# One small load on another queue, silu on another engine, and a new order of a written-out schedule

## The chip, the core and the metric

The kernel runs on one core of one Trainium2 chip. A core has five engines that run at the same time, each through its own list of instructions: TensorE (PE in the profile) multiplies matrices and writes to PSUM, VectorE (DVE), ScalarE (ACT) and GpSimd (POOL) work element by element, and SyncE (SP) issues the DMA transfers. They wait for each other by semaphores. The metric is the time of one execution on the device in microseconds (us).

## What is computed

One transformer block with adaptive layer norm, linear attention and a gated feed-forward part, on 2048 tokens of 512 channels, all in bfloat16:

```python
mod = (_silu(c) @ w_mod).reshape(c.shape[0], 6, 1, -1)
sa, ca, ga, sb, cb, gb = ...
h = _layernorm(x) * (1 + ca) + sa
x = x + ga * A(h)          # attention, 32 heads of 16 channels
h = _layernorm(x) * (1 + cb) + sb
x = x + gb * B(h)          # (silu(h @ w_gate) * (h @ w_up)) @ w_down, 1376 wide
```

In A, queries and keys go through a small matrix per head, `w_phi` (32 matrices of 16 by 16, 16 KB in all). phi of each is softmax(p) and softmax(-p) side by side, and the attention is num / den with num = phi_q (phi_k^T v) and den = phi_q (sum of phi_k). There is no product of tokens with tokens.

## The kernel before

**Staging.** Weights and all activations stay in SBUF. The 2048 tokens are 16 tiles of 128, in four chunks of x (`x_ch`). The stages are: preparation; K tiles (`k_tile`, `kv_tile`), which accumulate the key-value sums of all 16 tiles in `kv_ps`; Q tiles (`q_tile`); then, tile by tile, attention (`attend_tile`), its projection and second layer norm (`project`, `second_T`), and the feed-forward part (`ffn_gu`, `ffn_tail`, `ffn_down`) in six units of tokens. Stages overlap.

**Preparation**, which the change is mostly about:

- `c` is loaded through ACT's queue. Four products with a 1 by 1 matrix (`f_cT`, L450) turn it into a column in PSUM; ACT makes exp(-c) (L459); `f_silu` makes silu(c) with three operations of VectorE (L454 to L456).
- `mod_cols` (L471 and L473) multiplies silu(c) with the first third of `w_mod` as its four row blocks land, and a copy (L478) gives `modA`, the shift and scale of the first layer norm.
- `f_phx` (L499) spreads `w_phi` with 16 products of 16 columns, and VectorE makes the block-diagonal matrix `BD` from the result in PSUM (L502).
- `fold_phi` multiplies BD into the key weights (and later the query weights): 16 transposes of `wk` (L519), copies of them out of PSUM (L523), products with BD (L530), and copies back (L533, L534).
- `first_norm` takes the statistics of a tile of x (L348, L349), makes 1/sqrt(var) either by Ln and Exp of ACT (L377, L378) or by a power of GpSimd (L381, L382), and normalizes (L392, L396, L398 by engine). `turn_first` and `modulate_T` transpose (L563, L414) and apply modA on the way out of PSUM (L566, L567, L422).
- The first K product (L619) needs the folded wk and the modulated tokens.

**What sets the order.** Nothing is left to a scheduler of the compiler. Every step is recorded as an `Op` of a `Plan`, with what it reads and writes, an assumed duration (`us=`) and sometimes several engines to choose from (`alts`; "DVE*" is a VectorE operation that the plan keeps from running beside GpSimd). Loads recorded by `later` carry a size `kb` that the plan turns into a landing time, and a `Buf` with `at=` counts as ready at that time. The list `ORDER` gives the order in which the ops are placed: an entry divided by 4 is the op, and the remainder is the engine chosen. `Plan.run` walks it, gives each op a planned start, and the program is emitted in order of the planned starts. So the durations, sizes and `at=` in the code are assumptions that shape the order of instructions on each engine; on the chip the semaphores decide.

**Loads.** SP issues in this order: x chunk 0, wk, w_phi, w_mod (two row blocks, then one, then one), the two halves of x chunk 1, x chunk 2, wq, wv, x chunk 3, then transposes and the later weights.

**Filler.** Where the plan sees PE idle, `fill` puts products of a matrix of ones into the gap, which nothing reads; they keep PE busy. In the early part the number of columns is the gap times 1200 columns per us where the gap starts before 7.0 us, and 2400 behind it.

```python
left = int((o.start - t0) * (1200 if t0 < 7.0 else 2400))
while left >= 128:
    fns.append(lambda n=min(left, CW): f(n))
    left -= CW
```

## Time and profile before

| what | value |
|---|---|
| median of 3 runs | 199.06 us (199.02 to 199.08) |
| the profiled execution, its own time | 199.18 us |
| its span, first to last instruction | 197.4 us |
| granted TensorE clock | 1.000 of full speed |
| bytes read from and written to HBM | 11.58 MB and 2.10 MB |

The page of a profile shows, for each engine, the busy time, the groups of instructions that cost most, and the chain of work that ended last: from the last instruction back to what released each step. Besides it one can ask who waited for whom, what ran in a stretch of time, and when each transfer landed. In a line such as "L519 PE", the number is the line of the kernel. A stretch lists the busy time of PE, PEld (weight loads of PE), DVE, ACT and POOL, each with its number of instructions, then the granted clock, the busy share of the 16 DMA engines, and GB/s. Times in the text are from the start of the span.

When the first loads were issued and when they landed, by the trace:

| load | KB | issued by SP, us | landed, us |
|---|---|---|---|
| x chunk 0 | 512 | 0.72 | 4.1 |
| wk | 512 | 1.18 | 6.01 |
| w_phi | 16 | 1.65 | 6.2 |
| w_mod, row blocks 0 and 1 | 512 | 2.19 | 8.11 |
| w_mod, row block 2 | 256 | 2.7 | 8.79 |
| w_mod, row block 3 | 256 | 3.1 | 9.44 |

### The profile page before, as it was taken

The page shows a single profiled execution, that of the slowest core. Times are in us where ns is not written, and L with a number is a line of the kernel's source. Part 1 is how long each engine was busy: PE and PEld are TensorE (multiplying, and loading weights), DVE is VectorE, ACT ScalarE, POOL GpSimd, SP SyncE. Part 2 cuts the span into 40 slices and gives each one's busy share as a digit, 9 for nine tenths or more (in the row PEclk, how much of TensorE's full clock was granted, in tenths as well). Part 3 has the DMA queues.
Part 4 walks back from the last instruction along what each step waited for, and adds up shares of the span by engine and source line. Part 5 has one row for each costly group of instructions (what it writes and reads, how often), then busy time and mean ns, then how long its engine had stood idle before and what let it go on. Part 6 is the DMA issues. An engine that isn't in the chain of part 4 may idle for free.

```text
span 197.4 us, 4080 instructions
## 1 busy us (share of the span) xinstructions
PE 192.4 (97%) x1494; PEld 108.1 (55%) x1494; DVE 136.3 (69%) x268; ACT 108.9 (55%) x247; POOL 126.0 (64%) x207
## 2 busy tenths in 40 slices
PE   7999999999999999999999999999999999999993
PEld 2754555555754777967664555554444544544452
DVE  5999999999999899998973873844234203241453
ACT  2499999999769974366452452633145330134300
POOL 1469999999997667686763777657746420139200
DMA  6999789899928570836509157150370001021112
GB/s 203 334 381 151 129 201 355 186 310 392 203 53 162 107 151 13 167 66 110 99 14 188 37 100 82 30 130 0 66 103 20 27 0 53 3 66 40 47 38 76
DMA packets 51141, 24.16 MB, mean 122 GB/s; under 512 B 42449, under 2 KB 47922, under 8 KB 51122
## 3 DMA queue, kind: packets, MB, share of 16 engines
q1 hardware_dynamic: 50976, 23.88, 51.7%
q8 instruction: 11, 0.18, 0.4%
q14 instruction: 8, 0.07, 0.1%
q10 hardware_dynamic: 146, 0.03, 0.1%
HBM read 11.58 MB, written 2.10 MB: 69 GB/s over the span
## 4 chain that ended last, share of the span: by engine, by line
PE 93%; DMA 3%; DVE 1%; issue 1%; SPq 0%; DVEq 0%
PE one_ps L909 35%; PE one_ps L987 17%; PE one_ps L857 7%; PE one_ps L623 7%; PE one_ps L686 7%; PE one_ps L619 7%; PE one_ps L955 3%; DMA wk<-in_A_wqkv_dram 2%; PE kv_ps L663 2%; PE kv_ps L824 2%; PE kv_ps L1054 1%; DMA out_dram<-ot 1%; PE one_ps L530 1%; PE one_ps L473 1%; DVE fg L997 1%; PE one_ps L414 1%
## 5 line engine op out<-in xcount | busy, mean ns | idle before, releaser
L909 PE MATMUL one_ps<-hT,wgu_sb 128*128 128x512 bf16 (+2 forms) x480 | 74.5, 308 | 0.0
L909 PEld LDWEIGHTS <-wgu_sb 128*128 128x128 bf16 x480 | 40.3, 98 | 28.7
L916 ACT ACTIVATE sg<-one_ps 128x512 bf16<-128x512 f32 (+1 forms) x41 | 23.6, 586 | 37.2 <-PE one_ps L909 24.9
L987 PE MATMUL one_ps<-wd_sb,gu 128*128 128x512 bf16 (+1 forms) x160 | 37.8, 372 | 0.0
L925 POOL TENSOR_TENSOR gu<-usb,sg 128x512 bf16<-128x512 bf16 x19 | 22.1, 1168 | 24.2 <-ACT sg L916 12.2
L997 DVE TENSOR_TENSOR fg<-one_ps,gab 128x512 bf16<-128x512 f32 (+1 forms) x16 | 10.4, 667 | 23.8 <-PE one_ps L987 23.8
L919 DVE TENSOR_TENSOR gu<-one_ps,sg 128x512 bf16<-128x512 f32 (+1 forms) x22 | 14.2, 658 | 18.1 <-PE one_ps L909 11.1
L987 PEld LDWEIGHTS <-gu 128*128 128x128 bf16 x180 | 16.6, 98 | 16.0
L348 DVE BATCH_NORM_STATS2 st<-x_c 128x6 f32<-128x512 bf16 x32 | 21.3, 678 | 1.7 <-DMA x_c<-in_A_x_dram 1.5
L923 ACT CAST usb<-one_ps 128x512 bf16<-128x512 f32 x19 | 11.1, 586 | 18.2 <-PE one_ps L909 18.0
L640 DVE TENSOR_REDUCE S<-e 128x64 f32<-128x1024 bf16 x16 | 19.2, 1202 | 0.4 <-POOL e L657 0.2
L694 DVE TENSOR_REDUCE Sq<-eq 128x64 f32<-128x1024 bf16 x16 | 19.2, 1203 | 0.0
L690 ACT ACTIVATE eq<-one_ps 128x512 bf16<-128x512 f32 x32 | 17.1, 614 | 2.3 <-PE one_ps L686 2.2
L634 ACT ACTIVATE e<-one_ps 128x512 bf16<-128x512 f32 x32 | 17.0, 615 | 0.0
L657 POOL TENSOR_TENSOR e<-e,S 128x512 bf16<-128x512 bf16 x16 | 16.8, 1060 | 0.2
L857 PE MATMUL one_ps<-wo_sb,oT 128*128 128x512 bf16 x64 | 16.1, 379 | 0.0
L623 PE MATMUL one_ps<-wv,hT 128*128 128x512 bf16 x64 | 15.9, 379 | 0.0
L619 PE MATMUL one_ps<-wk,hT 128*128 128x512 bf16 x64 | 15.5, 379 | 0.0
L686 PE MATMUL one_ps<-wq,hT 128*128 128x512 bf16 x64 | 15.4, 379 | 0.0
L701 POOL TENSOR_TENSOR eq<-eq,Rq 128x512 bf16<-128x512 bf16 x14 | 14.8, 1059 | 0.4
L1001 POOL TENSOR_TENSOR ot<-x_c,fg 128x512 bf16<-128x512 bf16 x7 | 8.1, 1153 | 10.0 <-DVE fg L997 10.0
L860 DVE TENSOR_TENSOR x_c<-x_c,one_ps 128x512 bf16<-128x512 bf16 x16 | 10.7, 669 | 5.3 <-PE one_ps L857 5.1
(120 smaller groups left out, 279.7 us busy)
## 6 DMA issues: line engine op xcount, KB each, us to landing
wmod_sb<-in_w_mod_dram SPq DMA_DIRECT2D x2, 1024.0 KB, 7.8
out_dram<-ot SPq DMA_DIRECT2D x15, 128.0 KB, 1.9
x_c<-in_A_x_dram SPq DMA_DIRECT2D x3, 512.0 KB, 7.2
wgu_sb<-in_B_w_up_dram SPq DMA_DIRECT2D x1, 1376.0 KB, 10.9
wgu_sb<-in_B_w_gate_dram SPq DMA_DIRECT2D x1, 1376.0 KB, 13.4
wd_sb<-in_B_w_down_dram SPq DMA_DIRECT2D x1, 1280.0 KB, 7.5
wk<-in_A_wqkv_dram SPq DMA_DIRECT2D x1, 512.0 KB, 4.8
wmod_sb<-in_w_mod_dram SPq DMA_DIRECT2D x1, 512.0 KB, 5.9
```

The costliest lines, as they stand in the source:

```text
L348: pl.op("DVE", r=reads, w=[st6], us=0.6, fn=lambda: nc.vector.bn_stats(st6()[:], src))
L619: nc.tensor.matmul(pk()[:], lhsT=hT[c_i][k][:, cols], rhs=Wk2[:, k, :], start=(k == 0), stop=(k == KD - 1))
L623: nc.tensor.matmul(v()[:], lhsT=hT[c_i][k][:, cols], rhs=wv_sb[:, k, :], start=(k == 0), stop=(k == KD - 1))
L640: pl.op("DVE", r=[e], w=[Ss], us=1.13, fn=lambda: nc.vector.tensor_reduce(Ss()[:].rearrange("p g s h -> p (g s h)"), e()[:].rearrange("p g ...
L686: nc.tensor.matmul(pq()[:], lhsT=hT[c_i][k][:, cols], rhs=Wq2[:, k, :], start=(k == 0), stop=(k == KD - 1))
L690: pl.op("ACT", r=[pq, btab], w=[be[sg]], us=0.48, fn=lambda sg=sg: nc.scalar.activation(eq[:, :, sg].rearrange("p g h f -> p g (h f)"), pq ...
L694: pl.op("DVE", r=be, w=[Sq], us=1.13, fn=lambda: nc.vector.tensor_reduce(Sq()[:].rearrange("p g s h -> p (g s h)"), eq[:].rearrange("p g s ...
L857: nc.tensor.matmul(a()[:], lhsT=oT()[:, j0 + j, :], rhs=wo_sb[:, j, :], start=(j == 0), stop=(j == KD - 1))
L909: nc.tensor.matmul(ps_()[0:fsz, q * n:(q + 1) * n], lhsT=wgu_sb[:, k, i, m * P:m * P + fsz], rhs=h2[k], start=(k == 0), stop=(k == KD - 1))
L916: pl.op("ACT", r=[g, btab], w=[sg], us=0.08 + 0.41 * L / CW, fn=lambda: nc.scalar.activation(sg()[0:fsz, 0:L], g()[0:fsz, 0:L], ACT.Silu))
L925: pl.op("POOL", r=[usb, sg], w=[gu], us=0.17 + 0.98 * L / CW, fn=lambda: nc.gpsimd.tensor_tensor(gu()[0:fsz, 0:L], usb()[0:fsz, 0:L], sg() ...
L987: nc.tensor.matmul(fp()[:], lhsT=b()[0:fsz, c0:c0 + P], rhs=wd_[0:fsz, m, wcs], start=(m == 0), stop=(m == FM - 1))
```

## The change

It does five things.

1. w_phi is loaded by GpSimd's own queue, behind the first constants that GpSimd sets, and no longer by SP. The plan takes it as there at 5.4 us.
2. silu(c) is made by GpSimd: ACT copies c out of PSUM (`c_sb`) ahead of its Exp; GpSimd adds 1 (and caps the result at 1e38), takes the power -1 and multiplies.
3. f_phx's result is first copied to SBUF (`ph_sb`, by ACT in the new order), so that BD can be made by GpSimd, as it is in the new order.
4. The early filler is counted at 1200 columns per us up to 4.9 us and 2300 behind it.
5. ORDER is new, and with it the engines chosen; so are the sizes that the plan assumes for the loads. In the program it gives, SP's loads are x chunk 0, wk, w_mod (three parts), the first half of x chunk 1, x chunk 2, the second half of x chunk 1, wq, wv, x chunk 3. The later weights are reordered as well (w_gate and w_up apart from each other, the large part of w_down behind three transposes of Q).

`stats_act` isn't used, since ACT_STATS is empty. With EARLY = 1 the reciprocal of tile 0 in `attend_tile` may be made by ACT, and in the new order it is.

```diff
+ACT_STATS = ()
+ACC = 0.8
+EARLY = 1
 FILL_FROM, FILL_TO, FILL = 1.3, 90.0, 0.85
+WARM = 4.9
...
+    mone = const.tile([P, KD], FP32, name="mone")
+    nc.gpsimd.memset(mone[:], -1.0)
     eps_t = const.tile([P, 1], FP32, name="eps")
     nc.gpsimd.memset(eps_t[:], LN_EPS)
+    nc.gpsimd.dma_start(wphi_sb[:], A_w_phi.rearrange("h (q t) f -> (h q) (t f)", t=4))
...
-    bc, bphi = Buf(at=3.0), Buf()
+    bc, bphi = Buf(at=3.0), Buf(at=5.4)
...
-    later(x_ch[0][:], x_v[0], bx[0:4], 400)
-    later(Wk2[:], wqkv_v[:, :, D:2 * D], bwk[0:1], 690)
-    later(wphi_sb[:], A_w_phi.rearrange("h (q t) f -> (h q) (t f)", t=4), [bphi], 70)
-    for k, n, kb in ((0, 2, 770), (2, 1, 280), (3, 1, 280)):
+    later(x_ch[0][:], x_v[0], bx[0:4], 470)
+    later(Wk2[:], wqkv_v[:, :, D:2 * D], bwk[0:1], 600)
+    for k, n, kb in ((0, 2, 600), (2, 1, 245), (3, 1, 245)):
...
+    def f_sig():
+        nc.scalar.copy(c_sb[:], cT()[:])
+        nc.scalar.activation(sig[:], cT()[:], ACT.Exp, scale=-1.0)
+
     def f_silu():
-        nc.vector.tensor_scalar_add(sig[:], sig[:], 1.0)
-        nc.vector.reciprocal(rsig[:], sig[:])
-        nc.vector.tensor_tensor(silucT[:], rsig[:], cT()[:], op=ALU.mult)
+        nc.gpsimd.tensor_scalar(sig[:], sig[:], 1.0, 1e38, op0=ALU.add, op1=ALU.min)
+        nc.gpsimd.tensor_tensor(rsig[:], sig[:], mone[:, 0:KD], op=ALU.pow)
+        nc.gpsimd.tensor_tensor(silucT[:], rsig[:], c_sb[:], op=ALU.mult)
...
-    pl.op("ACT", r=[cT], w=[bsig], us=0.1, fn=lambda: nc.scalar.activation(sig[:], cT()[:], ACT.Exp, scale=-1.0))
-    pl.op("DVE*", r=[bsig, cT], w=[bsil], us=0.5, fn=f_silu)
+    pl.op("ACT", r=[cT], w=[bsig], us=0.3, fn=f_sig)
+    pl.op("POOL", r=[bsig], w=[bsil], us=1.5, fn=f_silu)
...
-    pl.op("DVE", r=[phx], w=[bBD], us=0.6, fn=lambda: nc.vector.tensor_tensor(
-        BD[:], phx()[:].rearrange("p (j f) -> p j f", f=DH).unsqueeze(2).to_broadcast([P, KD, 8, DH]),
-        bm128[:].unsqueeze(1).to_broadcast([P, KD, 8, DH]), op=ALU.mult))
+    pl.op([("ACT", 0.14, lambda: nc.scalar.copy(ph_sb[:], phx()[:])),
+           ("DVE", 0.13, lambda: nc.vector.tensor_copy(ph_sb[:], phx()[:]))], r=[phx], w=[bph])
+
+    def f_bd(eng):
+        eng.tensor_tensor(BD[:], ph_sb[:].rearrange("p (j f) -> p j f", f=DH).unsqueeze(2).to_broadcast([P, KD, 8, DH]),
+                          bm128[:].unsqueeze(1).to_broadcast([P, KD, 8, DH]), op=ALU.mult)
+    pl.op([("POOL", 1.05, lambda: f_bd(nc.gpsimd)), ("DVE*", 0.6, lambda: f_bd(nc.vector))], r=[bph], w=[bBD])
...
+        def fa():
+            nc.scalar.activation(A()[:], ndv()[:, :, HG:NDW], ACT.Ln)
+            nc.scalar.activation(A()[:], A()[:], ACT.Exp, scale=-1.0)
+        if n < EARLY:
+            alts.append(("ACT", 0.43, fa))
...
-            left = int((o.start - t0) * (1200 if t0 < 7.0 else 2400))
+            left = int(1200 * (min(o.start, WARM) - min(t0, WARM)) + 2300 * (max(o.start, WARM) - max(t0, WARM)))
```

## The prediction

> **What bounds the kernel now.** The profiled execution took 199.18 us, of which the span is 197.4; the median of the runs is 199.06. I work with differences against the profiled execution and subtract them from the median. I read first the busy table, then who waited for whom on TensorE, then the chain that ended last, then stretches of 1 us at the start.
>
> ```profile
> PE 192.4 (97%) x1494; PEld 108.1 (55%) x1494; DVE 136.3 (69%) x268; ACT 108.9 (55%) x247; POOL 126.0 (64%) x207
> ```
>
> TensorE (PE) is busy 97%. The waits of PE are only two in the whole run:
>
> ```profile
> PE kv_ps L1054 <- DVE ones L296: 1.4, 1, 1.4
> PE one_ps L519 <- DMA wk<-in_A_wqkv_dram: 0.4, 1, 0.4
> ```
>
> The columns are the total, the number and the longest. The first is the start, the second ends at 6.06 us, when wk has landed. After that PE waits for nothing until its last matmul at 194 us. So from 6.06 us on the time is a plain sum: the matmuls that compute something (1468 in both programs) plus the filler products (L1054), plus a tail of copies and stores that the change leaves as it is. Only three things can move the end: when the first transposes of wk start, how much filler stands behind them, and any new wait.
>
> The chain at that place:
>
> ```profile
> 1.18 4.83 DMA wk<-in_A_wqkv_dram
> 6.01 0.05 issue
> 6.06 0.40 PE one_ps L519 x4
> 6.46 0.38 PE one_ps L499 x16
> 6.84 0.69 PE one_ps L519 x12
> 7.53 0.65 PE kv_ps L1054 x3
> 8.17 0.22 PE one_ps L530 x4
> ```
>
> L519 transposes wk, L499 is the 16 products of w_phi (f_phx), L1054 is filler. w_phi's 0.38 us stands behind the first transposes, on the path.
>
> The loads, by stretches of 1 us (last two columns: busy share of the DMA engines, GB/s):
>
> ```profile
> 4.00:5.00 1.00, 1.00 (x4) 0.30 (x3) 0.87 (x2) 0.00 (x0) 0.00 (x0) 1.00 1.04 338
> 5.00:6.00 1.00, 0.69 (x4) 0.20 (x2) 1.00 (x4) 0.00 (x0) 0.00 (x0) 1.00 0.93 132
> 6.00:7.00 1.00, 0.94 (x26) 0.94 (x27) 0.86 (x6) 0.00 (x0) 0.67 (x2) 1.00 0.95 365
> ```
>
> From 5 to 6 us the engines look busy but move a third of the bytes. In the trace's packets, w_phi's 128 packets of 128 B run there, and directly behind them ten of w_mod's 2048-byte packets take 0.43 to 1.08 us each, where the later ones take 0.084: 8.7 us of engine time, about 7.9 more than normal, or 0.49 us of all 16 engines. It is a hole in the stream; it stands exactly where w_phi stands in SP's queue.
>
> **The change, part by part.**
>
> *w_phi's products ahead of wk's.* In the new order of instructions the 16 products stand ahead of all 16 transposes. PE then has six fillers of 512 columns behind the c products; in before the same six ran from 3.45 to 5.46. From 5.46 the products take 0.38, to 5.84, in time that was idle (the wait for wk). The path loses 0.38 us, if w_phi is there by about 5.65. When it comes through GpSimd's queue the trace of before can't show. The issue stands behind three small memsets, at about 1.6 us. Lower end: ACT's one load, 1 KB, landed 1.26 us after its issue (0.72 to 1.98): 2.9 us. Upper end: w_phi's own row of now, 4.5 us, most of it spent behind 1 MB in SP's queue: 6.1 us. Its size is w_phi's, its place (an empty queue) is that of ACT's load; I take a landing before 5.5, as the 4.5 us are mainly the queue. At 6.1 the cost is 0.45.
>
> A sentence of the Trainium skill's page "DMA: Bandwidth & Descriptors" (section "Anatomy of one DMA — SWDGE (gpsimd) path") would give an estimate of 2.0 us plus 16 KB at 436 GB/s, a landing near 3.6; the sum is the same by it.
>
> *SP's queue.* Without w_phi (0.50 us of issue, L289) the w_mod loads go out 0.54 earlier, and the hole of 0.49 is not between wk and w_mod. Bounds: w_mod's parts land as now (first pair 8.11, third 8.79, fourth 9.44), or up to 0.5 earlier. I take earlier. Behind them x's third chunk now stands between the halves of the second; the second half lands one 512 KB load later, some 1.4 us at 365 to 390 GB/s, near 11.5 to 12, and VectorE's new order takes its statistics last of the three. wq's issue now waits for wk to land (6.03, against 6.01); with one load fewer ahead of it that wait goes to x's first chunk, at 4.1, so it is earlier too.
>
> Against this part speaks the same page's section "Issuing engines are not separate DMA queues": all queues share the 16 engines, and another issuer saves issue time alone. By that rule the hole would remain in the stream, and the sum would be rival 1 below; the packet rows show what the hole hangs on, not whether it moves along.
>
> *Filler.* Counted in the built programs, behind the first of w_phi's products and wk's transposes: 15 fillers of 6588 columns before, 13 of 5597 after. Up to the first K products the two are equal (4804 and 4790 columns); the saving is behind them, where 1784 becomes 807. At 512 columns in 0.216 us (L619, eight in 1.73), 991 columns are 0.41 us. All of it is on PE, and so on the path, as long as the data are there. The two-rate count itself removes only the seventh early filler (142 columns), in idle time: nothing.
>
> *silu and BD on GpSimd.* silu on VectorE ended at 6.69 behind the statistics (L454 starts at 6.07, though its input was there at 3.7); its first use is at 8.44. On GpSimd: 0.24 (row L381), 0.72 (the pow of L382), 0.26 (L648) = 1.2 us from 3.9, when GpSimd is idle (its 4.9 us wait ahead of L381): done by 5.2. BD took 0.67 on VectorE and ended at 7.88. On GpSimd it lies between that 0.67 and the 1.17 of L925; the nearest row is L657, the same broadcast product, 1.06. From 6.1 (products at 5.84, then a 0.2 us copy on ACT) it ends at 7.2. Behind it wait the normalizations of x (L398), whose statistics come no earlier than 7.2. Cost 0, covered by idle time; VectorE loses 0.48 + 0.67 + 0.40 (one normalization goes to GpSimd). If a later w_phi held BD by 0.5, the normalizations would slip by the same.
>
> *The reciprocal of tile 0 on ACT* (0.52 by L644 and L645, for 0.34 on VectorE) falls near 55 us, where ACT idles 0.9 to 1.3 us at a time for PE. 0.
>
> *Does the data keep up?* PE: transposes 6.06 to 7.15, filler to 7.80, half of w_mod's products to 8.38 (needs w_mod's first pair: 8.11 now, 7.6 with the earlier stream), three folds of wk 9.05, the rest of w_mod 9.43, the last fold 9.67. modA is copied by 9.83. Then ACT is the longest: its last copy of wk 9.87 to 10.4, and three modulations at 0.5 each, to 11.9. PE comes to its first K product at 12.19 − 0.38 = 11.81. It waits 0.1: I count it. Later VectorE, ACT and GpSimd are 97 to 100% busy from 16 to 46 us, so they could hold PE when it comes earlier; but summing the rows of the new order up to the last K tile, VectorE has 0.2 less work, ACT about 1.0 more, of which 0.9 (the two copies, a Ln and Exp) falls in its idle time before 7 us, and GpSimd 1.8 more, against 2.3 of silu and BD that fill idle time before 7.3. At 54 us ACT already waits for PE, so it had slack. 0, with a doubt that is rival 3.
>
> **Sum**: −0.38 − 0.41 + 0.1 = −0.69 us: 199.06 − 0.7 = 198.35 (the profiled execution 198.5).
>
> **Rivals.**
> 1. *The hole goes where w_phi goes.* Its packets then delay x and wk: wk 0.49 later, at 6.5. The sum is −0.69 + 0.45 = −0.25: 198.8, which is no difference. For it: the same 16 engines. Against: they would then meet wk's stream, whose packets change at 3.5 us from those of x without a hole. If instead wk is on time and only w_mod comes as now, PE waits 8.11 − 7.80 = 0.31: 198.65.
> 2. *Slower: w_phi at the head of PE's queue comes late.* The 16 products stand ahead of all transposes, and PE runs in order; all fillers behind are fixed work that absorb nothing. Place: the first product. Each us of landing beyond 5.65 is a us of the end, so the gain is gone at 5.65 + 0.69 = 6.35. If GpSimd can complete its issue only when VectorE's opening run ends (2.6) and the load then takes its 4.5 us, it lands at 7.1: 199.06 − 0.69 + (7.1 − 5.65) = 199.8. For it: no load of GpSimd is in the trace. Against: 3 us of room between the lower end and 5.65.
>    For this the skill's page "DMA: Bandwidth & Descriptors", section "SWDGE vs HWDGE vs iDMA", names a reason: GpSimd writes its descriptors to SBUF, where VectorE can lock it out. Nothing in this trace shows that.
> 3. *The saving is given back later*, by a wait of PE between 16 and 60 us of some 0.5, as three engines there are full: 198.85. The less filler there is, the less such a wait is covered.
>
> **Chances.** Forecast 0.60; rival 1 0.15; rival 3 0.13; rival 2 0.12. A measurement can tell about 0.2%, 0.4 us, from no change, so faster means below 198.66. The forecast counts as faster, with a little of rival 1: 0.62; rivals 1 and 3 as same: 0.26; rival 2 as slower: 0.12. The range: low end 197.9, if w_phi is early, no wait appears and wk lands 0.3 earlier (13 of its 16 parts are there by 5.53, the last at 6.01); high end 199.2, which takes in rivals 1 and 3 with the upper landing of 6.1 and leaves out rival 2.
>
> **What would show it.** PE's w_phi products start before wk's transposes, near 5.5, and those near 6.0; no stretch of 1 us at the start with high DMA share and low GB/s; w_mod's products near 7.8 without a wait; the first K product near 11.9, against 12.19; PE's waits list with no new line over 0.2. If the transposes start after 6.4, or PE waits for w_phi's load, the prediction is wrong there; if the first K product is early and the end isn't, rival 3 is right.

## The result and the profile after

The changed kernel takes 201.93 us (median of 4 runs, 201.42 to 203.30), the kernel before 199.07 on the same chip: a ratio of 1.0142, 95% interval 1.0113 to 1.017. The forecast was 198.35 and its range ended at 199.2. The ratios here and below leave out executions in a slower state of the chip (two of five in e2, two of ten in e4, one each in e13 and e15); the medians are of all. The profiled execution of the changed kernel took 201.86 us, its span is 199.9.

The busy table of the changed kernel:

```profile
PE 193.1 (97%) x1491; PEld 108.0 (54%) x1491; DVE 138.0 (69%) x268; ACT 109.2 (55%) x251; POOL 127.5 (64%) x208
```

PE's share is the same 97%, in a span that is 2.5 us longer. The list of PE's waits (total, number, longest) says more:

```profile
PE kv_ps L1097 <- DVE ones L300: 1.4, 1, 1.4
PE one_ps L511 <- DMA wphi_sb<-in_A_w_phi_dram: 1.1, 1, 1.1
PE kv_ps L860 <- DVE KVZ L828: 0.6, 1, 0.6
PE one_ps L1030 <- DMA gut<-gul: 0.2, 1, 0.2
```

The wait for wk is gone, and three new ones stand there: for w_phi at the start, for KVZ near 56 us, and for a transpose by DMA near 79 us. The start on PE (start, length, line; in brackets the idle time before it):

```profile
3.45 2.74 PE L1097 MATMUL kv_ps<-ones 128*128 128x512 bf16 x6
7.31 0.55 PE L511 MATMUL one_ps<-wphi_sb,spread 128*128 128x16 bf16 x16 [1.11 <-DMA wphi_sb<-in_A_w_phi_dram]
7.71 1.05 PE L537 MATMUL one_ps<-ident_b,wk 128*128 128x128 bf16 x16
...
9.45 0.55 PE L485 MATMUL one_ps<-silucT,wmod_sb 128*128 128x1 bf16 x16
...
13.42 0.38 PE L655 MATMUL one_ps<-wk,hT 128*128 128x512 bf16 x1
```

w_phi's products start at 7.31, where the forecast had 5.46, and wk's transposes behind them at 7.71, in place of 6.06, though wk had landed at 5.60. The first K product starts at 13.42 (12.19 before). The load and the stretch from 5 to 6 us, each from its own view of the changed kernel:

```profile
wphi_sb<-in_A_w_phi_dram POOLq DMA_DIRECT2D x1, 16.0 KB, 5.8
```
```profile
5.00:6.00 1.00, 1.00 (x3) 0.30 (x2) 1.00 (x3) 0.00 (x0) 0.49 (x2) 1.00 0.95 307
```

GpSimd issues it at 1.50 and it lands 5.8 us later. In the packets of the trace it is 16 packets of 1024 bytes where SP's queue sent 128 of 128. They run from 5.87 to 6.75: all of wk's packets have started by 5.17, and 133 packets of w_mod, which SP issued later (1.65), start ahead of the first of them. The hole of before isn't in this trace (307 GB/s, 132 before), yet w_mod's parts land at 8.03, 8.69 and 9.34, 0.08 to 0.10 earlier than before.

Near 56 us on VectorE and GpSimd (two stretches of the timeline):

```profile
54.90 1.25 DVE L816 TENSOR_TENSOR wo_sb<-wo_sb,gab 128x512 bf16<-128x512 bf16 x1
56.07 0.18 DVE L826 SCALAR_TENSOR_TENSOR KVZ<-kv_ps,bm4z 128x32 bf16<-128x32 f32 x1
56.17 0.68 DVE L828 TENSOR_TENSOR KVZ<-kv_ps,bm 128x512 bf16<-128x512 f32 x1
```
```profile
54.71 2.45 POOL L816 TENSOR_TENSOR wo_sb<-wo_sb,gab 128x512 bf16<-128x512 bf16 x2
```

In the kernel before all four scalings of w_o (L780) are GpSimd's. In the new order one is VectorE's, directly ahead of KVZ, for which PE waits. The planner counts 0.34 us for it; beside GpSimd's own scaling it takes 1.25. The change is in the order's numbers (the remainder modulo 4 picks the engine), not in a line of code.

Where the 2.38 us went by which the last matmul is later, by three marks on PE in this and all following traces (us; the sign ° marks a kernel that leaves one scaling out; e2's profiled execution, 206.03 us, isn't in the table):

| kernel | first K product | first KVZ product | last matmul | K to KVZ | KVZ to last |
|---|---|---|---|---|---|
| before | 12.19 | 55.04 | 193.97 | 42.85 | 138.93 |
| changed | 13.42 | 56.90 | 196.35 | 43.48 | 139.45 |
| e1 | 12.49 | 55.72 | 195.03 | 43.23 | 139.31 |
| e3 | 12.70 | 56.06 | 195.80 | 43.36 | 139.74 |
| e5 | 12.73 | 55.22 | 195.74 | 42.49 | 140.52 |
| e9 | 12.15 | 54.77 | 195.28 | 42.62 | 140.51 |
| e10 | 12.01 | 54.62 | 194.59 | 42.61 | 139.97 |
| e13° | 15.08 | 57.61 | 197.20 | 42.53 | 139.59 |
| e14° | 11.82 | 54.49 | 194.25 | 42.67 | 139.76 |
| e4 | 12.20 | 54.97 | 193.90 | 42.77 | 138.93 |
| e6 | 12.58 | 55.32 | 194.49 | 42.74 | 139.17 |
| e7 | 12.23 | 54.98 | 193.90 | 42.75 | 138.92 |
| e8 | 13.43 | 56.17 | 195.10 | 42.74 | 138.93 |
| e11 | 12.23 | 55.02 | 193.94 | 42.79 | 138.92 |
| e12 | 11.78 | 55.12 | 194.05 | 43.34 | 138.93 |
| e15 | 11.82 | 55.45 | 194.38 | 43.63 | 138.93 |
| e16 | 11.85 | 55.60 | 194.53 | 43.75 | 138.93 |
| e17 | 12.72 | 55.46 | 194.39 | 42.74 | 138.93 |
| e18 | 11.28 | 54.47 | 193.40 | 43.19 | 138.93 |

The changed kernel loses 1.23 ahead of the first K product, 0.63 from there to KVZ, 0.52 behind it. The forecast had 11.9 for the first mark and 181.37 (181.78 less 0.41) from it to the end.

By the starts of PE's products, the 0.63 is 0.41 less filler (977 columns fewer) and 1.04 more waiting: 0.74 ahead of KVZ, and 0.31 at 43.74, where PE's weight load waits for GpSimd:

```profile
PEld L699 <- POOL e L693: 0.6, 1, 0.6
```

Of the 0.52 behind KVZ, 0.34 is the wait for the transposed tile (`gut`) near 79 us and 0.2 stands ahead of a product with w_o near 67 us. The profiled execution is 2.68 longer than that of before; the 0.3 that these marks don't hold lie behind the last matmul or outside the span.

### The profile page after: what moved, and what is told of

The parts are those of the page before. It is cut to its first block, busy times and chain, and to the rows that moved or that the text cites. A ratio compares the mean times of both kernels' runs of the same rounds, so it can differ in the third digit from the quotient of the medians.

```text
span 199.9 us, 4078 instructions
## 1 busy us (share of the span) xinstructions
PE 193.1 (97%) x1491; PEld 108.0 (54%) x1491; DVE 138.0 (69%) x268; ACT 109.2 (55%) x251; POOL 127.5 (64%) x208
## 4 chain that ended last, share of the span: by engine, by line
PE 58%; ACT 6%; DMA 3%; DVE 3%; issue 0%; DVEq 0%
PE one_ps L952 33%; PE one_ps L1030 16%; PE one_ps L900 4%; ACT eq L726 4%; PE one_ps L998 2%; DMA gut<-gul 2%; PE kv_ps L860 1%; PE one_ps L722 1%; DMA out_dram<-ot 1%; DVE Sq L730 1%; ACT hT L429 1%; ACT L713 1%; DVE ot L1044 0%; ACT sg L959 0%; DVE fg L1040 0%; DVE gu L962 0%
## 5 line engine op out<-in xcount | busy, mean ns | idle before, releaser
L959 ACT ACTIVATE sg<-one_ps 128x512 bf16<-128x512 f32 (+1 forms) x41 | 23.1, 586 | 35.7 <-PE one_ps L952 34.8
L1030 PE MATMUL one_ps<-wd_sb,gu 128*128 128x512 bf16 (+1 forms) x160 | 39.0, 372 | 0.0
L355 DVE BATCH_NORM_STATS2 st<-x_c 128x6 f32<-128x512 bf16 x32 | 20.9, 675 | 1.5 <-DMA x_c<-in_A_x_dram 1.5
L655 PE MATMUL one_ps<-wk,hT 128*128 128x512 bf16 x64 | 16.0, 379 | 0.0
L659 PE MATMUL one_ps<-wv,hT 128*128 128x512 bf16 x64 | 15.6, 379 | 0.0
L722 PE MATMUL one_ps<-wq,hT 128*128 128x512 bf16 x64 | 15.6, 379 | 0.0
L737 POOL TENSOR_TENSOR eq<-eq,Rq 128x512 bf16<-128x512 bf16 x14 | 14.8, 1062 | 0.3
L366 POOL TENSOR_SCALAR ln_neg<-ln 128x1 f32<-128x1 f32 x16 | 3.7, 233 | 12.5 <-DVE ln L356 11.7
```

Source lines behind the costliest of these rows:

```text
L355: pl.op("DVE", r=reads, w=[st6], us=0.6, fn=lambda: nc.vector.bn_stats(st6()[:], src))
L722: nc.tensor.matmul(pq()[:], lhsT=hT[c_i][k][:, cols], rhs=Wq2[:, k, :], start=(k == 0), stop=(k == KD - 1))
L959: pl.op("ACT", r=[g, btab], w=[sg], us=0.08 + 0.41 * L / CW, fn=lambda: nc.scalar.activation(sg()[0:fsz, 0:L], g()[0:fsz, 0:L], ACT.Silu))
L1030: nc.tensor.matmul(fp()[:], lhsT=b()[0:fsz, c0:c0 + P], rhs=wd_[0:fsz, m, wcs], start=(m == 0), stop=(m == FM - 1))
```

## The experiments

Ratios are against the kernel before on the same chip, whose median was 199.25 to 199.40 in these series.

### Which queue, and how late is w_phi (e1 to e4)

**e1**: the changed kernel, w_phi on ScalarE's queue.

```diff
     nc.scalar.dma_start(c_row[:], c[:, :])
+    nc.scalar.dma_start(wphi_sb[:], A_w_phi.rearrange("h (q t) f -> (h q) (t f)", t=4))
...
-    nc.gpsimd.dma_start(wphi_sb[:], A_w_phi.rearrange("h (q t) f -> (h q) (t f)", t=4))
```

> The changed kernel with one edit: w_phi is loaded by ACT's queue, right behind c, instead of GpSimd's. All orders of instructions stay. Theory (the late landing of w_phi, 7.31 us, at the head of PE's queue is the cause, and PE's later waits of 1.55 us follow from it): w_phi lands before 5.6, the transposes of wk start near 6.0 instead of 7.69, and the later waits go too: 201.9 - 1.7 - 1.5 = about 198.7. Rival (the new order carries the later waits in itself): only the head is gained, about 200.2. Rival (the landing isn't the cause): no change, 201.9.

Measured: 200.72 us, ratio 1.0070 (1.0047 to 1.0093). PE's waits of e1:

```profile
PE kv_ps L1097 <- DVE ones L301: 1.4, 1, 1.4
PE kv_ps L860 <- DVE KVZ L828: 0.6, 1, 0.6
```

w_phi lands at 5.2 and nothing waits for it, so about half of the loss comes with w_phi's way through GpSimd's queue; the wait for KVZ stays at the same size. The new order carries that one by itself.

**e2**: the changed kernel, w_phi in SP's queue between wk and w_mod, as before; its products still first.

```diff
-    later(Wk2[:], wqkv_v[:, :, D:2 * D], bwk[0:1], 600)
+    def f_wk_phi():
+        nc.sync.dma_start(Wk2[:], wqkv_v[:, :, D:2 * D])
+        nc.sync.dma_start(wphi_sb[:], A_w_phi.rearrange("h (q t) f -> (h q) (t f)", t=4))
+    pl.op("XBAR", w=list(bwk[0:1]), us=0.5, kb=600, fn=f_wk_phi)
```

> The changed kernel with w_phi loaded by SP between wk and w_mod, where it was before the change. Theory: it lands near 6.2, so PE's first product of w_phi is at 6.2 instead of 7.31: 1.1 less, 200.8 if the later waits stay, near 199.4 if they follow from the lateness. The hole of 0.5 us in the stream between 5 and 6 us is back. Rival (the landing isn't the cause): 201.9.

Measured: 200.91 us, ratio 1.0061 (1.0037 to 1.0086): within its interval the same as e1. The profiled execution took 206.03 us, far from that median, so its trace isn't read here.

**e3**: the changed kernel, GpSimd's load ahead of its constants.

```diff
     nc.scalar.dma_start(c_row[:], c[:, :])
+    nc.gpsimd.dma_start(wphi_sb[:], A_w_phi.rearrange("h (q t) f -> (h q) (t f)", t=4))
...
-    nc.gpsimd.dma_start(wphi_sb[:], A_w_phi.rearrange("h (q t) f -> (h q) (t f)", t=4))
```

> The changed kernel with GpSimd's load of w_phi as its first instruction of the body, ahead of the identity matrix: issued at 0.72 instead of 1.50. If the 5.8 us from issue to landing belong to this queue by itself, it lands 0.8 earlier, at 6.5, and the time is about 201.1. If its packets stand behind the 1 MB of x and wk that SP has issued by then, the landing stays near 7.2 and the time at 201.9. If an early issue gets ahead of x, it lands near 3.5 and the time is as with ACT's queue.

Measured: 200.82 us, ratio 1.0079 (1.006 to 1.0098). Issued at 1.22 it landed at 6.55, 5.3 us later; PE waited 0.9 for it.

**e4**: the kernel before, w_phi by GpSimd behind its constants; order and products as before.

```diff
-    later(wphi_sb[:], A_w_phi.rearrange("h (q t) f -> (h q) (t f)", t=4), [bphi], 70)
+    pl.op("XBAR", w=[bphi], us=0.5, kb=70, fn=lambda: nc.gpsimd.dma_start(
+        wphi_sb[:], A_w_phi.rearrange("h (q t) f -> (h q) (t f)", t=4)))
```

> The kernel before with this part of the change alone: w_phi loaded by GpSimd's queue behind its constants. In this order four transposes of wk stand ahead of w_phi's products. If the landing near 7.3 repeats, PE waits at the products from 6.5 to 7.3: 0.8 to 0.9 more, 199.9, plus later waits if the other engines are held as well; the hole between 5 and 6 us in the stream is gone. If the landing is before 6.4, no change or 0.1 less: 199.0.

Measured: 200.42 us, ratio 1.0086 (1.0047 to 1.0125), its runs from 199.25 to 202.44. The profiled execution was the fastest, with w_phi at 5.94, 4.5 us from the issue, and hardly a loss. What the median loses (1.1 us) isn't in this trace. The same load thus took 5.8, 5.3, 4.5 and (in e13) 6.2 us in four traces; on ScalarE's queue it took 4.0 to 4.6 in eleven. No queue brings it in the 1.26 us of ScalarE's first load, c.

### The kernel before, one part at a time (e6 to e8)

**e6**: w_phi on ScalarE's queue, behind c; SP issues nothing in its place.

```diff
+    nc.scalar.dma_start(wphi_sb[:], A_w_phi.rearrange("h (q t) f -> (h q) (t f)", t=4))
...
-    later(wphi_sb[:], A_w_phi.rearrange("h (q t) f -> (h q) (t f)", t=4), [bphi], 70)
+    pl.op("XBAR", w=[bphi], us=0.5, kb=70, fn=lambda: None)
```

> The kernel before with one edit: w_phi goes out on ScalarE's queue behind c, SP issues nothing in its place. It prices the load alone. Theory (a queue that is served at once, and no hole between wk and w_mod): w_phi lands near 5.2, wk near 5.75 in place of 6.01, no stretch of 1 us below 200 GB/s; the first transposes come 0.25 earlier, and w_mod's products, 8.44 in before, are held only by w_mod's first pair (8.1): 0.2 to 0.3 below the kernel before. Rival (the engines' total of bytes sets wk's and w_mod's landings, whoever issues): wk at 6.0 and the time within 0.2 of the kernel before.

Measured: 199.64 us, ratio 1.0005 (0.9993 to 1.0018). The rival holds: with ScalarE in place of SP as the issuer, nothing moves that can be measured.

**e7**: e6, and w_phi's products ahead of wk's transposes.

```diff
-    pl.op("PE", r=[bphi], w=[phx], us=0.42, fn=f_phx)
+    pl.op("PE", r=[bphi], w=[phx], us=0.42, fn=lambda: None)
+    ahead = [f_phx]
...
                 def ft(i=i, tp=tp):
+                    if ahead:
+                        ahead.pop()()
```

> The run before with one more edit: the 16 products of w_phi stand ahead of the first transposes of wk on PE, as the change has them. Nothing else of the order moves. Theory of the forecast (0.38 us of products put into the wait for wk): with w_phi there by 5.3 and six and a bit fillers to about 5.6, the products run before wk lands; transposes near 6.0 and no products behind them: 0.3 to 0.4 below the load-alone run, as far as w_mod's first pair (8.1) allows; 198.8 to 199.0 where the kernel before takes 199.2. Rival (w_mod's landing takes back what is gained at the start): PE then waits at its first w_mod product (L473's like) by as much, and the time stays within 0.1 of the load-alone run.

Measured: 199.31 us, ratio 0.9994 (0.9984 to 1.0003). The products run from 5.64, the transposes from 6.04 with nothing between, as forecast, and the first K product is at 12.23 (before 12.19). A new wait of PE:

```profile
PE one_ps L535 <- DVE ln_nmr L385: 0.5, 1, 0.5
```

The named instruction stands directly behind BD on VectorE. BD runs there from 7.33 to 8.0, as it stands behind a statistic and silu, and the first fold (L535) needs it. What the early products gained, 0.4 us at the transposes, is given back by what is late next; neither the forecast of w_mod's products nor my rival for this run named it.

**e8**: the kernel before, silu and BD on GpSimd; w_phi in SP's queue, old order.

```diff
-        nc.vector.tensor_scalar_add(sig[:], sig[:], 1.0)
-        nc.vector.reciprocal(rsig[:], sig[:])
-        nc.vector.tensor_tensor(silucT[:], rsig[:], cT()[:], op=ALU.mult)
+        nc.gpsimd.tensor_scalar(sig[:], sig[:], 1.0, 1e38, op0=ALU.add, op1=ALU.min)
+        nc.gpsimd.tensor_tensor(rsig[:], sig[:], mone[:, 0:KD], op=ALU.pow)
+        nc.gpsimd.tensor_tensor(silucT[:], rsig[:], c_sb[:], op=ALU.mult)
...
+    def f_bd():
+        nc.scalar.copy(ph_sb[:], phx()[:])
+        nc.gpsimd.tensor_tensor(BD[:], ph_sb[:]...
+    pl.op("DVE", r=[phx], w=[bBD], us=0.6, fn=f_bd)
```

> The kernel before with silu and BD on GpSimd as in the change (c copied by ScalarE, power on GpSimd; w_phi's products copied by ScalarE, BD by GpSimd ahead of the normalizations), in the old order and with w_phi in SP's queue. Theory of the forecast (these cost nothing, they lie in idle time): within 0.2 of the kernel before. Rival (BD is 0.5 us longer on GpSimd and one copy and one crossing later, so it comes at about 8.7 in place of 7.88; PE's first fold, L530, at 8.17 in before, waits for it, and the normalizations behind it on GpSimd are late in turn): PE waits 0.4 to 0.6 for BD; 0.4 to 0.8 above the kernel before.

Measured: 200.48 us, ratio 1.0053 (1.0035 to 1.007). The wait, and ScalarE and GpSimd ahead of it (three views of e8):

```profile
PE one_ps L542 <- POOL BD L514: 1.1, 1, 1.1
```
```profile
7.26 0.59 ACT L535 COPY WT<-one_ps 128x512 bf16<-128x512 bf16 x1 [3.47 <-PE one_ps L531]
7.74 0.22 ACT L513 CAST ph_sb<-one_ps 128x64 bf16<-128x64 f32 x1
```
```profile
8.04 1.16 POOL L514 TENSOR_TENSOR BD<-ph_sb,bm 128x512 bf16<-128x512 bf16 x1 [0.76 <-ACT ph_sb L513]
```

w_phi's products are done by 6.84. Their copy stands behind a copy of wk on ScalarE and comes at 7.74; BD takes 1.16 (0.67 on VectorE) and ends at 9.2. The rival holds, at more than its price. The first fold starts at 9.25, 1.10 later than in e12 (8.15), where PE's rate doubled at the same moment (see the last section); against the kernel before the first K product is 1.24 later. In the new order the folds stand behind half of w_mod's products, and neither e1 nor the changed kernel waits for BD; there this cost is covered.

### Is the filler on the path (e11, e12)

**e11**: the kernel before without the 1784 columns of filler behind the first K products. **e12**: also without the 1310 directly ahead of them (11.5 becomes 11.0).

```diff
         if early:
+            if t0 > 11.5:
+                return
             left = int((o.start - t0) * (1200 if t0 < 7.0 else 2400))
```

> The kernel before without the 1784 columns of filler that stand behind the first K products (nothing else differs). It prices by itself the term of the forecast that counted fewer filler columns as time on the path. Theory of the forecast (all filler is on PE and so on the path): 1784 columns at 512 in 0.216 us are 0.75 us less: first K product to last matmul 181.0, time 0.6 to 0.75 below the kernel before. Rival (the filler stands where PE would wait for evictions or normalizations anyhow): a wait of PE of 0.3 to 0.75 appears between 13 and 20 us, and the time is within 0.3 of the kernel before.

> The same without the 1310 columns directly ahead of the first K product as well (3094 columns less than the kernel before). Theory (they stand in a wait for the modulated x: ScalarE's third modulation ends at 11.9 to 12.1 when PE's first K product starts at 12.19): PE waits there, the first K product starts 0.1 to 0.3 earlier, and the time is 0 to 0.3 below the run without the filler behind. Rival (all of it on the path): 0.55 below that run. Rival (PE's clock falls when it waits): the time is above that run.

Measured: 199.48 us, ratio 1.0007 (0.9993 to 1.0021), and 199.35, 1.0000 (0.9989 to 1.0011). KVZ's first product is at 55.02 and 55.12, as before (55.04). In e11 the filler's 0.75 us come back as gaps between products, 0.19 to 0.33 each at 20.9, 23.3 and 24.7; the list of waits shows the largest:

```profile
PE one_ps L619 <- POOL hT L589: 0.2, 1, 0.2
```

e12's first K product is 0.41 earlier, and the first V product still stands at 15.74, behind a gap. In both, w_v's load lands 0.04 us ahead of that product (15.72 and 15.70), as in the kernel before (15.95, with V at 15.99). So in the kernel before the filler is not on the path: it stands where PE would wait. "PE busy 97%, no wait" was a picture that the filler paints.

### The late waits of the new order (e5, e9, e10, e13, e14)

**e5**: e1, the scaling of VectorE given to GpSimd in the same place.

```diff
-        pl.op([("POOL", 1.115, lambda fw=fw: fw(nc.gpsimd)), ("DVE*", 0.34, lambda fw=fw: fw(nc.vector))],
+        pl.op([("POOL", 1.115, lambda fw=fw: fw(nc.gpsimd)), ("DVE*", 0.34, lambda fw=fw: fw(nc.gpsimd))],
```

> The changed kernel with w_phi on ScalarE's queue behind c (as in the run before it), and the one scaling of w_o that the new order puts on VectorE directly ahead of KVZ given back to GpSimd (same place in the order, same filler; only the engine of that one instruction differs). Theory (the new order brings its own wait: VectorE's scaling takes 1.25 us beside GpSimd's and holds KVZ, for which PE waits 0.72): the wait ahead of L860 falls below 0.2 and the time by 0.6 to 0.7, from 200.7 to about 200.05. Rival (KVZ is late for its own inputs, or the fourth scaling on GpSimd makes the next user of w_o late): PE waits as long at the same place or at the first product of w_o; 200.5 to 200.8.

Measured: 200.15 us, ratio 1.0032 (1.0014 to 1.005). From K to KVZ 42.49 in place of 43.23: the scaling on VectorE cost 0.74 there. But a wait of the same size stands at w_o now:

```profile
PE one_ps L1030 <- DMA gut<-gul: 0.7, 1, 0.7
PE one_ps L900 <- POOL wo_sb L816: 0.6, 1, 0.6
```

Theory and rival both hold in part. **e9**: e5, with the fourth scaling directly behind the other three, ahead of the query product L737.

```diff
-        pl.op([("POOL", 1.115, ...
+        o = pl.op([("POOL", 1.115, ...
+        o.early = 2.0 if k == 0 else 0.0
...
-        for o in sorted(self.ops, key=lambda o: (o.start, o.n)):
+        for o in sorted(self.ops, key=lambda o: (o.start - o.early, o.n)):
```

> The run with w_phi on ScalarE's queue and all four scalings of w_o on GpSimd, with one more edit: the fourth scaling stands directly behind the other three, ahead of the query product L737 that the new order puts between (in the kernel before no such product stands between). Theory (the 0.6 to 0.77 us that PE waits at KVZ or, without VectorE's scaling, at the first product of w_o is the place of the scalings in the new order, nothing else): no wait of PE over 0.2 between 40 and 66 us; from the first K product to the last matmul 182.2 to 182.4 in place of 183.0, and the time 0.6 to 0.7 below that of the run it starts from (1.0032 of the kernel before): 0.9998. Rival (VectorE and GpSimd are both full up to here, so a wait of the same size comes a little later, at the query product that was moved back): the time stays near 1.003.

Measured: 200.49 us, ratio 1.0066 (1.0046 to 1.0086). The rival holds: the wait moves on to the query product that was put back, whose transpose is late:

```profile
PE kv_ps L861 <- DMA pT<-eq: 1.0, 1, 1.0
```

**e10**: e9, with the first product that reads gut one group of gate products (0.86 us) later.

```diff
+                late = n == 0 and m1 == FM
+                o = pl.op("PE", ..., fn=lambda m0=m0, m1=m1 - late, f=f: f(m0, m1))
+                o.after = (lambda f=f: f(FM - 1, FM)) if late else None
...
             fns.append(o.alt[2])
+            if o.eng == "PE":
+                if held:
+                    fns.append(held)
+                held = o.after
```

> The same with one more edit: the first down product that reads the transposed tile gut stands one group of eight gate products (0.86 us) later on PE; in the changed kernel PE waits 0.2 to 0.85 for that transpose by DMA, in the kernel before it comes 10 us later in the order. Theory (the new order's late waits are these two alone, and the 991 columns of filler are gone from the path as forecast): from the first K product to the last matmul 181.3 to 181.6, which is 0.2 to 0.5 below the kernel before (181.8), and a time 0.1 to 0.4 below that of the kernel before where the first K product is at 12.2. Rival (other places hold PE as soon as these are cleared): 182 or more, and the time not below the kernel before.

Measured: 200.32 us, ratio 1.0050 (1.0027 to 1.0073). The wait for gut is gone (KVZ to last 139.97, e9 140.51), the one for pT stays; the time is not below the kernel before.

**e13**: the changed kernel without VectorE's scaling. **e14**: e9 without the scaling that the order had given to VectorE.

```diff
-... ("DVE*", 0.34, lambda fw=fw: fw(nc.vector))],
+... ("DVE*", 0.34, lambda: None)],
```

> The changed kernel, w_phi by GpSimd as there, without the one scaling of w_o on VectorE (that quarter of w_o stays unscaled; nothing else differs). Theory (this scaling is in itself the wait ahead of KVZ: 1.25 us on VectorE, which runs without a gap from 9 us to KVZ): PE's wait of 0.58 ahead of L860 goes, from the first K product to the first product of KVZ it takes 42.5 to 42.7 us in place of 43.5, and the time falls by 0.7 to 0.9 from that of the changed kernel. Rival (something else of the new order holds KVZ): the wait stays over 0.4.

> The run with all four scalings on GpSimd ahead of the query product (there PE waited 1.13 at its fourth product of KVZ for pT), with the fourth scaling left out (that quarter of w_o stays unscaled; nothing else differs). Theory (GpSimd has one instruction of 1.1 us too many for what the new order asks of it by 62 us, so every place for it only moves the wait): the wait for pT falls under 0.2, from the first product of KVZ to the last matmul 139.3 to 139.5 in place of 140.5, time 0.9 to 1.1 below that run. Rival (SP's queue of transposes holds pT, not GpSimd): the wait stays over 0.5.

Measured, e14: 199.63 us, ratio 1.0016 (1.0004 to 1.0028). No wait for pT is left, the only new one is gut's:

```profile
PE kv_ps L1098 <- DVE ones L301: 1.4, 1, 1.4
PE one_ps L1031 <- DMA gut<-gul: 0.3, 1, 0.3
```

The first K product at 11.82 and the way from there to KVZ, 42.67, are together 0.55 shorter than in the kernel before, most of the forecast's 0.7; behind KVZ 0.83 is lost again, of which the list names 0.3. So the wait for KVZ is a matter of the amount of work: GpSimd has one instruction of 1.1 us too many for what the new order asks of it by 62 us, and VectorE can't take it cheaply. e13 in its trace does what the theory says (K to KVZ 42.53, no wait for KVZ; 0.95 less than the changed kernel, of which 0.31 is the wait at 43.74, which this execution doesn't have), but its time is no better: 202.56, ratio 1.0144 (1.012 to 1.0168). The start on PE in e13 says why:

```profile
7.75 0.58 PE L511 MATMUL one_ps<-wphi_sb,spread 128*128 128x16 bf16 x16 [1.56 <-DMA wphi_sb<-in_A_w_phi_dram]
8.18 1.87 PE L537 MATMUL one_ps<-ident_b,wk 128*128 128x128 bf16 x16
9.84 1.22 PE L1097 MATMUL kv_ps<-ones 128*128 128x512 bf16 x3
```

w_phi landed at 7.7, and behind the wait PE ran at half rate until about 10.7: 16 transposes took 1.87 us, 1.05 in the changed kernel's trace, where the rate had doubled by then behind a wait of 1.1. The first K product came at 15.08. The loss at the start is thus 1.2 us in one execution of the same start and 2.9 in another.

### Where an earlier start goes (e15 to e18)

**e15**: e7 with silu on GpSimd (as in e8; BD stays on VectorE). **e16**: e15 without the 3094 columns of e12.

> The kernel before with three parts: w_phi on ScalarE's queue behind c, its products ahead of wk's transposes, silu on GpSimd (BD stays on VectorE, which then starts it 0.5 earlier); all filler as before. Theory (from the first K products to KVZ VectorE is the bound, so only what makes VectorE's work less or starts it earlier counts): BD ends at 7.5, the first fold does not wait, first K product 11.8 to 11.9, and KVZ's first product at 54.5 to 54.7 in place of 55.0: 0.3 to 0.5 below the kernel before. Rival (the chain through GpSimd's normalizations or w_mod's landing is what counts): the first K product is earlier and KVZ is not; within 0.15 of the kernel before.

> The same without the 3094 columns of filler directly ahead of and behind the first K products. Theory (with VectorE earlier by 0.5 some of the filler comes to stand on the path): 0.1 to 0.3 below the run with the filler. Rival (VectorE still bounds the stretch, as in the two runs where the filler alone was taken away): the same within 0.1.

Measured: 199.35 us, ratio 1.0004 (0.9991 to 1.0016), and 199.36, 1.0008 (0.9992 to 1.0024). e15's fold no longer waits, and its first K product is at 11.82 as expected. Then:

```profile
16.40 1.02 PE L636 MATMUL one_ps<-wv,hT 128*128 128x512 bf16 x4 [0.72 <-DMA wv<-in_A_wqkv_dram]
```

w_v, issued at 6.0, lands 10.4 us later; the stream of loads holds the first V product, and neither my theory nor the rival had named it. In the kernel before w_v lands at 15.95 and V starts at 15.99: there too its landing is the limit, with filler in front (e11 and e12 show the same).

**e17**: e15, and the load of x's fourth chunk behind wq's first transpose. **e18**: e17 without the 3094 columns.

```diff
+LATE = 7.0
...
     for c_i in (2, 3):
-        later(x_ch[c_i][:], x_v[c_i], bx[c_i * TPC:(c_i + 1) * TPC], 620)
+        o = later(x_ch[c_i][:], x_v[c_i], bx[c_i * TPC:(c_i + 1) * TPC], 620)
+        o.early = -LATE if c_i == 3 else 0.0
```

> The kernel before with w_phi on ScalarE's queue, its products first and silu on GpSimd (first K product at 11.82, but PE then waited 0.89 for w_v, which landed at 16.4), with one more edit: the load of x's fourth chunk, which SP issues at 8.0 and which then shares the engines with w_v until 16.4, goes out behind the first transpose of wq, at about 14.8. Theory (w_v's landing is what is late next; VectorE and GpSimd behind it follow): w_v lands near 15.0, V starts without a wait at 15.4 to 15.6, KVZ's first product at 54.4 to 54.7 in place of 55.0 to 55.4; time 0.3 to 0.5 below the kernel before. Rival (the transposes by DMA or the fourth chunk come later by as much, VectorE needs that chunk at 20.5): a new wait between 17 and 30 us, KVZ at 55.0 or later, the time not below the kernel before.

> The same without the 3094 columns of filler directly ahead of and behind the first K products. Theory (with the loads out of the way the filler comes to stand on the path, some 560 columns of it between K and V): 0.1 to 0.3 below the run with the filler. Rival (VectorE and GpSimd bound this stretch): the same within 0.1.

Measured: 199.26 us, ratio 0.9994 (0.9983 to 1.0005), and 199.13, 0.9989 (0.9978 to 1.0001). In both w_v lands 9.4 us from its issue, at 15.6 and 15.5. That holding the chunk back did this isn't shown: without it the load took 9.2 to 10.7 us in the nine other traces of the old order. In e18 V starts then, KVZ follows at 54.47 and the last matmul at 193.40, 0.57 earlier than in the kernel before. In e17's execution PE's rate doubled late (at 7.5 us, see the last section), and the first K product came only at 12.72. e18 is the best version found; its interval just takes in no change, and it can't be told from e17's.

## Why the prediction was wrong, step by step

1. **w_phi's landing** (the step that failed first): "Its size is w_phi's, its place (an empty queue) is that of ACT's load; I take a landing before 5.5, as the 4.5 us are mainly the queue". It landed at 7.3. ScalarE's queue was as empty, and the load took 4.0 to 4.6 us there in eleven traces, as in SP's (4.4 to 4.6); so an empty queue alone doesn't make it fast. On ScalarE's queue its packets start at 3.7 to 4.0, when those of x's first chunk are through or nearly (the last ends at 3.6 to 4.0), and ahead of most of wk's; c's load was over before x's. On GpSimd's queue they start at 4.8 (e3, e4), 5.2 (e13) and 5.9 (the changed kernel), behind nearly all of wk's 512 packets (452 or more), and in the last two behind part of w_mod's too, though that was issued later. What holds them back isn't shown. GpSimd's queue adds up to 1.6 us so. Both of my bounds, 2.9 and 6.1, lay below what came. The Trainium skill's "DMA: Bandwidth & Descriptors", section "Anatomy of one DMA — SWDGE (gpsimd) path", gave the estimate of 3.6; the four traces show 5.9 to 7.7, and they decide.

   What it cost: first K product 13.42 for 11.9. Not all of that is the load. The prediction took the six fillers ahead of w_phi's products to end at 5.46, as in before's trace; here they ran at half rate to 6.2 (the last section has the moments of all traces), and only from there PE waited 1.1 for w_phi. In e5, which has the same order up to the first K product, w_phi on ScalarE's queue and the doubling as late (7.7), that product is at 12.73, 0.69 earlier. In e14, with w_phi on ScalarE's queue and the doubling at 5.1, it is at 11.82: under their conditions the −0.38 and the 0.1 were right.
2. **SP's queue**: I read the hole as standing where w_phi stands in SP's queue. That was wrong. In e11 w_phi is in SP's queue, and from 5 to 6 us there is no hole; in e15 it is in ScalarE's, and there is one (the two stretches, e11 first):

```profile
5.00:6.00 1.00, 1.00 (x4) 0.30 (x2) 1.00 (x5) 0.00 (x0) 0.00 (x0) 1.00 1.01 345
```
```profile
5.00:6.00 1.00, 1.00 (x21) 0.66 (x20) 1.00 (x5) 0.00 (x0) 0.46 (x2) 1.00 0.78 172
```

   w_mod's first pair lands at 7.3 to 8.1 in the traces, and at 7.5 to 8.1 where w_phi is in SP's queue. What makes the hole isn't shown. The rule that I set against myself ("Issuing engines are not separate DMA queues", same page: another issuer saves issue time alone) was the better guide for ScalarE: e6 has 1.0005 (0.9993 to 1.0018). For GpSimd it isn't the whole: e4, where the issuer alone is changed, has 1.0086 (1.0047 to 1.0125).
3. **Filler, −0.41**: "All of it is on PE, and so on the path, as long as the data are there." The condition failed in the old order: e11 takes 1784 columns from the kernel before and gains nothing, as V still starts when w_v lands. In the changed kernel w_v is there at 14.95 and V starts at 17.40, so this limit doesn't stand there. In it the 0.41 was gained and 1.04 of waits came on top. With VectorE's scaling away, the way from K to KVZ is 42.49 to 42.67 against 42.85: 0.18 to 0.36 of the 0.41 arrived there, and was lost again behind KVZ.
4. **"From 6.06 us on the time is a plain sum"** was the reading behind 3. e7 shows the next late thing at once (BD on VectorE), e11, e12 and e15 the one behind it (w_v, at 15.7 and 16.4).
5. **silu and BD at 0**: in the new order nothing shows a cost, as the folds stand later; the 0.2 us copy of w_phi's products starts on ScalarE right behind them (7.89). In the old order the two cost 1.1 (e8 against e12), as ScalarE has a copy of wk ahead of that copy there, and BD takes 1.16 on GpSimd for 0.67 on VectorE. The pow took 1.05, not 0.72.
6. **"Later engines: 0"**: I summed VectorE's rows only up to the last K tile. The scaling of w_o, which the new order gives to VectorE, stands just behind, and no term held it: 0.74 (e5 against e1; e13's 0.95 takes in the 0.31 of another wait). The warning was in the profile of before: VectorE's products of 128x512 bf16 take 0.42 us in one group (L1001) and 1.01 in another (L701).
7. **gut**: the new order reads the first transposed tile at 79.6 in place of 90; the wait of 0.2 to 0.7 that comes of it (by the lists of six traces) was in no step.

In the profiled execution the forecast's −0.7 became +2.7. Of the difference, 1.52 lies ahead of the first K product (step 1), 1.04 from there to KVZ (0.7 by step 6, 0.3 by the wait for GpSimd at 43.74), 0.52 behind it (0.34 by step 7), and 0.3 behind the last matmul or outside the span.

Rival 2 named the place and nearly the landing (7.1), and gave 199.8. Its reason, that GpSimd can complete the issue only at 2.6, isn't shown: the issue ran from 1.50 to 2.29, and the packets start at 5.87. The rest are the waits of 6 and 7 and the one at 43.74. They lie partly where rival 3 looked, but in the changed kernel they are more than the saving given back. What stays open: why GpSimd's load takes 4.5 us in one execution and 6.2 in another, when PE's rate doubles, and what the median owes to each; my traces are one execution each. The reciprocal on ScalarE cost nothing that a run shows.

## What to carry to other kernels

Filler makes a waiting engine look busy, so before time on it is counted as path, take the filler away and see whether the marks move. A small load in a queue of its own isn't a fast one by that; before its first user is put at the head of an in-order engine, look in a trace of that very load when it lands. In a new order, read for every instruction which engine it now has, and what stands directly behind it, also where the source lines are unchanged.

## What the runs showed of the hardware

PE's rate doubles at a moment that differs from one execution to the next, with nearly the same work up to there: the spacing of products falls from 0.427 to 0.216 us (512 columns) or from 0.107 to 0.056 us (128 columns) at 4.7 (e10), 4.8 (e15), 4.9 (before), 5.0 to 5.1 (e3, e4, e7, e14), 5.3 (e18), 6.1 (e9, e11), 6.3 (e8, e12), 6.8 (e16), 7.2 (e1, e6), 7.5 (e17) and 7.7 us (e5), while the column of the granted clock shows 1.00 there. Where PE had waited 1.6 us before, it was about 10.7 (e13); in the changed kernel, behind a wait of 1.1, the rate had doubled by 7.7. The Trainium skill's page "TensorE: Matmul & The Clock Gate" (section "What's actually happening") lets the clock rise after a busy window of 3.4 us that runs freely, and expects the moment to vary by 0.5 us to either side; it varies by 3.0 us here. An estimate from that window: the first one that lies wholly in PE's work, which begins at 1.44, ends between 4.84 and 8.24, and all of these but the two earliest do.

Four traces have the same order up to the first K product and w_phi on ScalarE's queue: with the doubling at 5.1, 6.1, 7.2 and 7.7 that product starts at 11.82, 12.15, 12.49 and 12.73 (e14, e9, e1, e5; w_mod's first pair lands at 7.32 to 8.08 in them, too). The constant of 4.9 by which the changed kernel counts its filler is thus one draw of several, and the profile of before was an early one. The runs of the kernel before lie between 198.8 and 201.2 (one at 202.4); that this moment is what spreads them isn't shown.

A product of 128x512 bf16 on VectorE took 1.23 to 1.25 us while GpSimd ran the same kind (L816 in the changed kernel, e1 and e3), against 0.42 in the group L1001 of the kernel before. GpSimd's one beside which it ended took 1.33 there, its others 1.15 to 1.16.

GpSimd's queue packs w_phi's rows of 128 bytes into packets of 1024 (four traces); SP's and ScalarE's send 128 packets of 128. The stretch from 5 to 6 us moves 263 to 335 GB/s with GpSimd's queue, 172 to 368 with ScalarE's and 132 to 345 with SP's. In its three lowest (132 before, 158 in e8, 172 in e15) ten to twelve of w_mod's 2048-byte packets take 0.4 us or more, where 0.084 is usual; seven do in e4 with GpSimd's queue. No queue is free of them, and their cause isn't shown.
